# Thirty-five products that nobody reads, ahead of ten steps of a front written out by hand

## Chip, cores, metric

One core of a Trainium2 chip runs the whole program. The time is the device time of one execution in microseconds (us), and the figure given is the median of several runs. The engines are TensorE (PE in the rows; PEld are its weight loads), VectorE (DVE), ScalarE (ACT), GpSimd (POOL) and SyncE (SP, which issues most DMAs).

## What is computed

The reference is a block with two halves, cut here to its last lines:

```python
    x = A_u
    mod = (_silu(c) @ w_mod).reshape(c.shape[0], 6, 1, -1)
    sa, ca, ga, sb, cb, gb = (mod[:, 0], mod[:, 1], mod[:, 2], mod[:, 3], mod[:, 4], mod[:, 5])
    h = _layernorm(x, axis=-1) * (1 + ca) + sa
    x = x + ga * _A_ref(h, A_A_re, A_A_im, A_B_re, A_B_im, A_C_re, A_C_im, A_log_dt, A_Dskip)
    h = _layernorm(x, axis=-1) * (1 + cb) + sb
    x = x + gb * _B_ref(h, B_w1, B_w3, B_w2)
    return x
```

`_A_ref` is a state-space layer: for each of 640 channels a kernel K of 2048 steps is made out of 128 complex exponentials and is convolved with the layer's input by Fourier transforms. `_B_ref` is a gated feed-forward layer (640 to 1728 and back). The sequence has 2048 rows.

## The kernel before

The first layer has 40 steps (numbered s or k, 16 channels each). A step makes tables of exponentials (words `PA`, `PQ` on PE; `XA`, `XQ`, the phases `AB`, `CO`, `SI` on ScalarE; `E1`, `E2`, `A1`, `A2` on VectorE), multiplies and sums them on PE into K (`kg`, function `kgen`, into the PSUM tile `pk`), scales K on VectorE (`D`, `K`, functions `k_direct` and `k1evac`: from `pk` to the SBUF tile `K1`, named `K` in the rows), transforms it on PE (`pt`, function `k_stage1`, into the PSUM tile `pt`) and copies the result on ScalarE into `uk` (`uk`, function `k_out`). The tables E and the PSUM tiles are scarce: there are two buffers of E, one `pk` and one `pt` (its bank is called "pb"), so that a step of each kind waits for the reader of the step before.

Beside that, the 16 blocks of the input (`U+0` to `U+15`) are normalised on ScalarE (`LN`) and transformed on PE (`U`, function `u_products`, into two PSUM tiles `pu`, one in the banks "Z", the other in the banks "A" or "B", which the tables' products `pa` use too), and each half is taken out of PSUM by ScalarE or VectorE (`V0`, `V1`, function `u_out`).

The front of the program, about its first 122 us, is one hand-written list of words, `FRONT` (L1017). While it runs, every instruction of every engine is kept in the order of that list (class `InOrder`, L105; L115 is the line of its helper, and so the line of nearly all rows). Each engine takes its instructions strictly in that order, and an instruction that waits holds up all behind it on its engine. The list's end, around the change, reads:

```python
        "A2+4 V0+10 V1+10 kg+4 R7+2 LG+3 LN+7 K+4 PA+8 E1+5 uk+3 XA+8 pt+4 E2+5 A1+5 XA+9 uk+4 PA+10 A2+5 "
        "E1+7 XA+11 U+15 LN+6 V0+15 PH+8 V1+15 kg+5 U+13 XA+10 pt+2 AB+8 E1+6 V0+13 V1+13 K+5 A1+6 A1+7 E2+6 "
        "PQ+8 E2+7 uk+2 XQ+8 U+12 XQ+9 V0+12 V1+12 U+14 A2+7 CO+8 V0+14 kg+7 A2+6 pt+5 V1+14 CL+0 K+7 kg+6 "
        "PH+10 E1+8 SI+8 ul+0 ul+3 PQ+10 AB+10 E1+9 SI+10 K+6 uk+5 ul+1 XQ+11 pt+7 XQ+10 uk+7 E2+8 A1+9 CO+10 "
        "pt+6 A1+8 uk+6 E2+9 A2+8 A2+9 ul+2 kg+8 st+10 PH+12 K+8 "
```

After the front, rounds of the same words and of the convolution (`st`, PSUM tile `p` in the rows; `kc` takes it out on ScalarE) go to about 345 us, and the second layer, dense products on PE, runs to the end. Where the first layer ends the kernel already has 16 products of a tile of zeros that nobody reads (L1157, tile `idle`), 128x128 weights and 512 columns each.

Of the kernel before, what the change touches and what calls it, by code (L numbers as in the profile page):

```python
# [120 lines left out]
def tile_kernel(ctx: ExitStack, tc: tile.TileContext, a):  # L121
    nc = tc.nc
    V, S, G, PE = nc.vector, nc.scalar, nc.gpsimd, nc.tensor
# [19 lines left out]
    V, S, G, PE, Q = (InOrder(tc, e, (front,)) for e in (nc.vector, nc.scalar, nc.gpsimd, nc.tensor, nc.sync))  # L143

    def keep(ins):

        return tc.keep_in_program_order(ins) if in_order[0] else ins
# [48 lines left out]
    lx = once([P, KD, 4, P], F32R, "lx")  # L196
    r2 = once([P, 8, NB], F32R, "r2")
# [326 lines left out]
    def u_products(j):  # L524

        x = xt[j]
        ut[j] = pus = [psS.tile([P, 2, 512], F32, name="pu", tag=t, bufs=1) for t in ("Z", "AB"[j % 2])]
        for h in range(2):
            one = j % 2 == 0 and h == 0
            for q in range(2 if one else 0):  # L530
                for hh in range(2):
                    PE.matmul(pus[h][hh * 64:hh * 64 + 64, q, :320], c1[q * NA:q * NA + 1],
                              rrow[q * NA:q * NA + 1, hh * 320:hh * 320 + 320],
                              start=True, stop=False, tile_position=(q * NA, hh * 64))
            for q in range(2):
                r0 = (2 * h + q) * NA
                r = slice(r0, r0 + NA)
                for hh in range(2):
                    PE.matmul(pus[h][hh * 64:hh * 64 + 64, q, :320], s1r[r], x[r, hh * 320:hh * 320 + 320],
                              start=not one, stop=True, tile_position=(r0, hh * 64))  # L540
# [14 lines left out]


    LAG = SPC + 2

    ph, cs, AA, EC, PK, K1 = {}, {}, {}, {}, {}, {}

    pA, pQ = {}, {}

    banks = {"A": ("zt", LAG), "Z": None, "B": None}
    used = {}

    def two_banks(shape, name, release):

        free = [t for t, r in banks.items() if r is None or r in used]
        tag = min(free, key=lambda t: used.get(banks[t], -1))
        banks[tag] = release  # L570
        return psS.tile(shape, F32, name=name, tag=tag, bufs=1)
# [95 lines left out]
    def kgen(s):  # L667
        E, A = EC.pop(s), AA.pop(s)
        pk = psS.tile([P, SD // 4, NB], F32, name="pk", tag="pk", bufs=1)
        for g in range(SD // 4):  # L670
            for st, x in enumerate((E, A)):
                for dq in range(4):
                    keep(PE.matmul(pk[dq * 32:dq * 32 + 32, g, :], x[:, g * 4 + dq, 1, :], x[:, g * 4 + dq, 0:3:2, :],
                                   start=(st == 0), stop=(st == 1), tile_position=(0, dq * 32)))
        PK[s] = pk
# [14 lines left out]
    def k_stage1(s):  # L690
        pt = PT[s] = psS.tile([P, 4, P], F32, name="pt", tag="pb", bufs=1)
        kk = K1.pop(s)
        for g in range(4):
            for c in range(2):
                keep(PE.matmul(pt[c * 64:c * 64 + 64, g, :], kk[:, g, :], s1[:, c, :],
                               start=True, stop=True, tile_position=(0, c * 64)))
# [45 lines left out]
    def stage2(ch, g):  # L742
# [7 lines left out]
        if n:  # L750
            p2 = two_banks(shape, "p2", ("zt", n + LAG))
        else:
# [99 lines left out]
    def late_products(g):  # L852

        zt, w = ztl[g], i2bt[g - LATE].rearrange("p (f c) -> p f c", f=4)
        for f in range(4):
            for j in range(4):
                r = slice(j * 32, j * 32 + 8)
                end = keep_order(PE.matmul(pls[j][:, :P], w[r, f, :], zt[r, f, :],
                                           start=(g == LATE and f == 0), stop=(g == 7 and f == 3),
                                           skip_group_check=True, tile_position=(j * 32, 0)))  # L860
        return end
# [92 lines left out]
    def conv_part(fn):  # L954
        return lambda k: fn((k - LAG) // 8, (k - LAG) % 8)

    parts = {"PH": phases, "AB": absph, "CO": cosine, "SI": sine, "PA": lambda k: exp_fast((k,)), "XA": fast,
             "PQ": lambda k: exp_slow((k,)), "XQ": slow, "E1": real1, "E2": real2, "A1": imag1, "A2": imag2,
             "kg": kgen, "D": k_direct, "K": k1evac, "pt": k_stage1, "uk": k_out}
    conv = {"st": conv_part(stage2), "kc": conv_part(k_copy), "T": conv_part(products), "P": conv_part(products2), "Y": conv_part(sums),  # L960
            "iv": conv_part(inverse1), "zt": conv_part(z_store)}
# [3 lines left out]
    def do(name, k):  # L965

        lo, hi = (LAG, LAG + 8 * NDC) if name in conv else (0, NS)
        if name in by_two and k % 2:
            return None
        if front[0]:  # L970
            assert (name, k) not in done and lo <= k < hi, (name, k)
        if (name, k) in done or not lo <= k < hi:
            return None
        done.add((name, k))
        used[name, k] = len(used)
        return (conv if name in conv else parts)[name](k)
# [20 lines left out]
    def u_first(i):  # L997

        u_load(0, i)
        if i == 0:  # L1000
            ahead[0, 1, "s2"] = stage2_load(1)
            for g in range(2):
# [3 lines left out]
    once_only = lambda fn: lambda k: fn()  # L1006
    fronts = {"wl": mod_load, "xl": ln1_load, "ms": mod_first, "mc": mod_cols, "LS": ln1_stats, "LG": ln1_power, "LN": ln1_norm,
              "U": u_products, "V0": lambda k: u_out(k, 0),
              "V1": lambda k: u_out(k, 1), "SA": once_only(shift_a), "SB": once_only(shift_b), "SC": once_only(shift_c),
              "SD": once_only(shift_d), "MG": once_only(gate_a), "MH": once_only(gate_b), "dc": once_only(small_loads),  # L1010
# [38 lines left out]
    for word in FRONT:  # L1049
        name, k = word[:2].rstrip("+"), int(word[len(word[:2].rstrip("+")):])  # L1050
# [36 lines left out]
    for rnd in range(8 + 1):  # L1087
        if 2 <= rnd < 7:
            late_load(rnd - 2)
        for word in ROUND if rnd < 8 else LAST:  # L1090
            name, k = word.split("+")
            k = int(k) + (EB * rnd if rnd < 8 else 0)
# [13 lines left out]

    for tk in range(NS + 1, LAG + 8 * NDC + 2):
        do("st", tk)
        do("kc", tk)
        if tk == LAG + 8 * NDC:  # L1110
            end, made = late_products(6), []
# [66 lines left out]
    V, S, G, PE = (InOrder(tc, e, (in_order,)) for e in (nc.vector, nc.scalar, nc.gpsimd, nc.tensor))  # L1178
# [612 lines left out]
```

## Time and profile before

| | |
|---|---|
| time, median of 3 runs | 910.67 us (909.97 to 912.61) |
| the profiled execution's own time | 908.64 us |
| its span, first to last instruction | 906.8 us |
| mean granted TensorE clock | 0.971 of full speed |
| PE, DVE, ACT, POOL busy | 860.9, 686.3, 537.5, 275.4 us |

A share of busy time is an average over the front, the rounds and the second layer, which have different limits. PEclk is the clock that the chip granted to TensorE: 1.00 is 2.4 GHz and 0.50 is 1.2 GHz, and a value between them is a mean over a stretch that holds both. A matmul's row in the timeline is longer than the distance to the next one's start, since they overlap; costs are therefore read from starts. Products of 32-bit floats stand in the rows twice (x16 for 8 instructions); the type float32r stands once.

### The profile page before, as it was taken

Reading aid. Unit: us, or ns where it says so; the run is one execution under the profiler, and the core shown is the slowest. Engines: PE = TensorE matmul, PEld = TensorE weight load, DVE = VectorE, ACT = ScalarE, POOL = GpSimd, SP = SyncE. Lnnn points to the kernel's source line nnn. Section 1 sums busy time; section 2 is a strip of 40 time slices with the busy share of each in tenths; the row PEclk is TensorE's granted clock in tenths of the full one; section 3 lists DMA queues with packets and bytes.
Section 4 is the critical chain, followed back from the end, with each engine's and each line's share of the span. In section 5 each row is a group of like instructions: output and inputs, shape, how many; then the busy total and the mean of one; then the engine's idle time right before and its main releaser. Section 6 shows DMA issues by size and latency. Waiting matters only on the chain.

```text
span 906.8 us, 20206 instructions
## 1 busy us (share of the span) xinstructions
PE 860.9 (95%) x8082; PEld 660.1 (73%) x8082; DVE 686.3 (76%) x1210; ACT 537.5 (59%) x762; POOL 275.4 (30%) x315
## 2 busy tenths in 40 slices
PE   3788979999999999999999999999999999999997
PEld 2445557776666767788888887788888888888886
DVE  5899899999999968786666556867866766653664
ACT  6989899999999535554343324665534333323432
POOL 3342544554443030422222103300522222100662
PEclk9677699999999999999999999999999999999999
DMA  9655387676665887862211169736311311223352
GB/s 270 213 219 190 147 242 224 196 207 196 207 210 189 282 253 235 212 211 73 59 56 40 51 157 265 226 109 205 100 59 59 116 44 44 59 102 101 102 199 77
DMA packets 106017, 140.69 MB, mean 155 GB/s; under 512 B 19940, under 2 KB 65508, under 8 KB 105924
## 3 DMA queue, kind: packets, MB, share of 16 engines
q1 hardware_dynamic: 95796, 115.29, 42.0%
q10 hardware_dynamic: 8272, 18.16, 6.7%
q0 software_dynamic: 1856, 5.97, 2.0%
q8 instruction: 63, 1.03, 0.5%
q14 instruction: 30, 0.25, 0.1%
HBM read 107.92 MB, written 31.46 MB: 154 GB/s over the span
## 4 chain that ended last, share of the span: by engine, by line
PE 70%; ACT 12%; DVE 11%; DMA 3%; issue 3%; POOL 0%; DVEq 0%; SPq 0%; ACTq 0%
PE ps L115 60%; PE p L115 5%; ACT A L115 3%; DVE A L115 3%; ACT cs L115 3%; DVE E L115 2%; ACT L115 1%; DVE uk L115 1%; PE pk L115 1%; DMA zs<-zt 1%; ACT ph L115 1%; ACT uk L115 1%; PE pt L115 1%; PE pu L115 1%; DVE u L115 1%
## 5 line engine op out<-in xcount | busy, mean ns | idle before, releaser
L115 DVE TENSOR_TENSOR s<-ps,s 128x512 f32<-128x512 f32 x138 | 94.8, 687 | 83.1 <-PE ps L115 82.9
L115 ACT CAST gh<-rw 128x640 fp32r<-128x640 f32 x87 | 63.2, 727 | 110.0 <-PE ps L115 84.2
L115 DVE TENSOR_TENSOR gl<-rw,gh 128x640 fp32r<-128x640 f32 x87 | 77.2, 887 | 62.9 <-ACT gh L115 60.3
L115 POOL TENSOR_TENSOR S<-rw 128x256 f32<-128x256 f32 x46 | 36.1, 787 | 229.2 <-DVE S0l L115 156.2
L115 POOL TENSOR_TENSOR ph<-thi,iota 128x1376 int32<-128x1376 int32 x20 | 56.3, 2817 | 108.9 <-DVE A L115 35.3
L115 PE MATMUL ps<-xA,gh 128*128 128x512 f32 x280 | 87.5, 391 | 0.4 <-ACT xA L115 0.4
L115 PE MATMUL ps<-gh,uh 128*128 128x512 f32 x224 | 87.6, 391 | 0.0
L115 PE MATMUL ps<-gl,uh 128*128 128x512 f32 x224 | 87.4, 390 | 0.0
L115 DVE TENSOR_TENSOR E<-A,cs 128x1024 f32<-128x1024 f32 (+1 forms) x80 | 82.0, 1037 | 2.1 <-PE pk L115 1.5
L115 PE MATMUL ps<-gh,ul 128*128 128x512 f32 x208 | 81.2, 390 | 0.0
L115 PE MATMUL p<-uk,s 128*64 128x256 f32 x576 | 70.7, 386 | 2.6 <-ACT zt L115 1.1
L115 ACT ACTIVATE A<-pa 128x1024 f32<-128x1024 f32 (+1 forms) x80 | 64.6, 847 | 3.6 <-PE pa L115 3.1
L115 PEld LDWEIGHTS ps<-xA,gh 128*128 128x128 f32 x280 | 52.3, 188 | 12.6 <-ACT xA L115 0.7
L115 POOL TENSOR_TENSOR rw<-rw,gbr 128x128 f32<-128x128 f32 x56 | 35.7, 668 | 73.9 <-DMA rw<-in_w_dram 72.9
L115 PEld LDWEIGHTS p<-uk,s 128*64 128x64 f32 x576 | 38.7, 137 | 25.6 <-ACT A L115 3.3
L115 PE MATMUL ps<-xA,gl 128*128 128x512 f32 x140 | 54.6, 390 | 0.0
L115 ACT ACTIVATE s<-ps 128x512 f32<-128x512 f32 (+1 forms) x33 | 19.7, 596 | 49.9 <-PE ps L115 47.1
L115 PE MATMUL pt<-s,K 128*64 128x128 f32 x640 | 45.7, 287 | 3.4 <-ACT uk L115 3.0
L115 PEld LDWEIGHTS ps<-gh,uh 128*128 128x128 f32 x224 | 42.1, 188 | 8.9 <-DVE h L115 0.2
L115 PEld LDWEIGHTS ps<-gl,uh 128*128 128x128 f32 x224 | 42.1, 188 | 8.9
L115 DVE TENSOR_TENSOR A<-A,ph 128x1024 f32<-128x1024 f32 x40 | 48.5, 1216 | 0.0
L115 POOL TENSOR_TENSOR rs<-mv,epst 128x1 f32<-128x1 f32 (+1 forms) x17 | 6.0, 354 | 132.9 <-DVE mv L115 128.0
(224 smaller groups left out, 2220.1 us busy)
## 6 DMA issues: line engine op xcount, KB each, us to landing
rw<-in_w_dram ACTq DMA_DIRECT2D x44, 320.0 KB, 3.1
us<-u SPq DMA_DIRECT2D x16, 640.0 KB, 3.2
rw<-in_wg_dram SPq DMA_DIRECT2D x31, 320.0 KB, 2.7
s<-in_s_dram SPq DMA_DIRECT2D x36, 256.0 KB, 3.9
i<-in_i_dram SPq DMA_DIRECT2D x36, 256.0 KB, 4.5
rw<-in_wu_dram SPq DMA_DIRECT2D x28, 320.0 KB, 3.2
uk<-us SPq DMA_DIRECT2D x16, 512.0 KB, 4.9
zs<-zt SPq DMA_DIRECT2D x16, 512.0 KB, 4.3
```

Source lines behind the costliest of these rows:

```text
L115: ins = fn(*args, **kw)
```

## The change

A table names ten steps and a number for each. Ahead of such a step's products, PE makes that many products of two tiles that are long at hand, `lx` (as weights, 128 rows and 128 columns) and `r2` (512 columns, 256 where the bank has no more), into the very PSUM bank that the step's own products are about to overwrite. 21 of the 35 are 512 columns wide, and 14, those ahead of K products, are 256 wide. Nothing else is added, removed or moved.

```diff
@@ u_products(j)
         ut[j] = pus = [psS.tile([P, 2, 512], F32, name="pu", tag=t, bufs=1) for t in ("Z", "AB"[j % 2])]
+        idle_first("U", j, pus[0][:, 0])
@@
     LAG = SPC + 2
 
+    idle_products = {("U", 15): 2, ("kg", 5): 5, ("U", 13): 2, ("pt", 2): 2, ("U", 12): 2, ("U", 14): 3,
+                     ("kg", 7): 3, ("pt", 7): 4, ("pt", 6): 6, ("kg", 8): 6}
+
+    def idle_first(name, k, bank):
+        for _ in range(idle_products.get((name, k), 0)):
+            keep(PE.matmul(bank, lx[:, 0, 0, :], r2.rearrange("p j b -> p (j b)")[:, :bank.shape[1]], start=True, stop=True))
+
@@ kgen(s)
         pk = psS.tile([P, SD // 4, NB], F32, name="pk", tag="pk", bufs=1)
+        idle_first("kg", s, pk.rearrange("p g b -> p (g b)"))
@@ k_stage1(s)
         kk = K1.pop(s)
+        idle_first("pt", s, pt.rearrange("p g c -> p (g c)"))
```

PE's order in the changed program, from the last `pa` ahead of `U+15` to `pt+2`. In brackets are the engines that a row waits for (Activation is ScalarE); `r_98,lx` are the new products, and rows left out are the rest of `kg+5` and `U+13`.

```order
L115 MATMUL pa<-r_98,lx 128x512 [waits Activation_49]
L115 MATMUL pu<-r_98,lx 128x512 x2
L115 MATMUL pu<-x,misc 64x320 x4
L115 MATMUL pu<-x,misc 64x320 [waits Activation_49]
L115 MATMUL pk<-r_98,lx 128x256 x5
L115 MATMUL pk<-E 32x64 [waits DVE_49]
L115 MATMUL pu<-r_98,lx 128x512 [waits DVE_49]
L115 MATMUL pt<-r_98,lx 128x512 x2
L115 MATMUL pt<-s_74,K_938 64x128 x8
```

The steps keep their order; the new products stand ahead of each, and those of `U+13` take over the wait for VectorE that the step's own first product had.

PE's order before, from `PQ+10` to `kg+8` (`pt+7`, `pt+6`, then the first products of `kg+8`):

```order
L115 MATMUL pa<-r_99,lx 128x256 x4
L115 MATMUL pt<-s_74,K_1224 64x128 [waits Activation_49]
L115 MATMUL pt<-s_74,K_1224 64x128 x7
L115 MATMUL pt<-s_74,K_1286 64x128 [waits DVE_49,Activation_49]
L115 MATMUL pt<-s_74,K_1286 64x128 x7
L115 MATMUL pk<-E 32x64 [waits DVE_49]
L115 MATMUL pk<-E 32x64 x3
L115 MATMUL pk<-A 32x64 [waits DVE_49]
```

The same place in the changed program:

```order
L115 MATMUL pa<-r_99,lx 128x256 x4
L115 MATMUL pt<-r_98,lx 128x512 [waits Activation_49]
L115 MATMUL pt<-r_98,lx 128x512 x3
L115 MATMUL pt<-s_74,K_1243 64x128 x8
L115 MATMUL pt<-r_98,lx 128x512 [waits Activation_49]
L115 MATMUL pt<-r_98,lx 128x512 x5
L115 MATMUL pt<-s_74,K_1305 64x128 [waits DVE_49]
L115 MATMUL pk<-r_98,lx 128x256 x6
L115 MATMUL pk<-E 32x64 [waits DVE_49]
L115 MATMUL pk<-A 32x64 [waits DVE_49]
```

The wait for ScalarE, which frees the bank of `pt`, has gone from the transform's first product to the first new one, so the new products stand behind that wait and the transform stands behind them.

## Rows read from the trace of the kernel before

**Rows 1.** Busy time by stretch: us, engine busy (instructions), granted PE clock, DMA share, GB/s.

```profile
94.40:95.70 1.30, 1.05 (x12) 0.55 (x8) 1.30 (x3) 1.30 (x3) 0.00 (x0) 1.00 0.05 13
95.70:102.50 6.80, 6.80 (x106) 3.45 (x106) 5.98 (x7) 5.58 (x6) 5.15 (x3) 0.50 0.24 96
102.50:105.90 3.40, 2.69 (x44) 1.48 (x42) 3.37 (x6) 2.36 (x5) 1.30 (x1) 0.99 0.48 186
105.90:112.80 6.90, 6.90 (x102) 4.24 (x104) 5.56 (x10) 6.89 (x5) 3.28 (x2) 0.51 0.49 186
112.80:122.20 9.40, 5.07 (x170) 3.87 (x166) 7.97 (x11) 9.31 (x11) 2.88 (x3) 1.00 0.83 228
...
125.00:290.00 165.00, 162.16 (x3128) 115.02 (x3116) 161.05 (x278) 164.46 (x184) 77.27 (x41) 1.00 0.67 207
...
345.00:906.00 561.00, 555.33 (x2798) 452.31 (x2792) 374.25 (x647) 238.90 (x414) 139.20 (x214) 1.00 0.41 118
```

**Rows 2.** Timeline of PE: start us, us, line operation out<-in, [idle before <-releaser].

```profile
96.06 2.54 PE L115 MATMUL pu<-x,misc 32*64 32x320 f32 x16
...
98.52 0.44 PE L115 MATMUL pk<-E 128*32 128x64 f32 x8
...
100.39 1.37 PE L115 MATMUL pu<-x,misc 32*64 32x320 f32 x16
101.69 1.49 PE L115 MATMUL pt<-s,K 128*64 128x128 f32 x16
...
106.89 2.60 PE L115 MATMUL pu<-x,misc 32*64 32x320 f32 x16
109.42 0.44 PE L115 MATMUL pk<-E 128*32 128x64 f32 x8
...
111.29 1.80 PE L115 MATMUL pt<-s,K 128*64 128x128 f32 x16
113.02 0.32 PE L115 MATMUL pk<-E 128*32 128x64 f32 x8
...
114.05 0.39 PE L115 MATMUL pa<-r,lx 32*128 32x256 f32 x4
115.71 1.09 PE L115 MATMUL pt<-s,K 128*64 128x128 f32 x16 [1.26 <-ACT uk L115]
118.58 1.09 PE L115 MATMUL pt<-s,K 128*64 128x128 f32 x16 [1.78 <-ACT uk L115]
119.60 0.32 PE L115 MATMUL pk<-E 128*32 128x64 f32 x8
121.10 0.32 PE L115 MATMUL pk<-A 128*32 128x64 f32 x8 [1.18 <-DVE A L115]
```

**Rows 3.** Timeline of ACT: the idle time of 95 to 124 us and what follows it.

```profile
103.22 0.58 ACT L115 COPY uk<-pt 128x512 f32<-128x512 f32 x1 [1.70 <-PE pt L115]
...
105.09 0.69 ACT L115 COPY u<-pu 128x640 f32<-128x640 f32 x1 [0.29 <-PE pu L115]
...
115.09 0.57 ACT L115 COPY uk<-pt 128x512 f32<-128x512 f32 x1
...
117.93 0.59 ACT L115 COPY uk<-pt 128x512 f32<-128x512 f32 x1
...
121.66 0.56 ACT L115 COPY uk<-pt 128x512 f32<-128x512 f32 x1
...
124.27 0.59 ACT L115 COPY kc<-p 128x512 f32<-128x512 f32 x1 [0.23 <-PE p L115]
```

**Rows 4.** Timeline of DVE: its waits for PE in 109 to 123 us.

```profile
111.42 0.17 DVE L115 TENSOR_TENSOR pk<-pk,dz 128x4 f32<-128x4 f32 x1 [1.04 <-PE pk L115]
...
114.07 2.37 DVE L115 TENSOR_TENSOR E<-A,cs 128x1024 f32<-128x1024 f32 x1 [0.89 <-PE pk L115]
...
122.16 0.17 DVE L115 TENSOR_TENSOR pk<-pk,dz 128x4 f32<-128x4 f32 x1 [0.51 <-PE pk L115]
```

**Rows 5.** Timeline of PE: the sixteen products of zeros that the kernel has already.

```profile
350.03 3.92 PE L115 MATMUL ps<-idle 128*128 128x512 f32 x16
```

## Prediction

> **What bounds the kernel now.** I read the stretches first, then the three engines' timelines around the change.
>
> The stretches show two falls of TensorE's clock where the new products go: 0.50 of full speed from 95.7 to 102.5 us and 0.51 from 105.9 to 112.8, with 0.99 between and 1.00 after [rows 1]. PE is busy for all of both low stretches, 6.80 of 6.80 and 6.90 of 6.90 us, so a busy PE did not keep the clock. Ahead of the first fall it was busy 1.05 of 1.30 us with small products on 32 rows and with `pt`. In the stretches it ran `pu` (32 rows), then `pk` and `pt` (128 rows), and each rise came behind those last [rows 2].
>
> What PE's pace costs shows on the others. ScalarE waits 1.70 us for `pt+2` and 0.29 for `U+12`; behind that, from 105.1 to 124.3, it has no gap [rows 3], and from 125 to 290 it is busy 164.46 of 165 us [rows 1]. VectorE waits 1.04, 0.89 and 0.51 us for `pk` [rows 4] and is then busy 161.05 of 165. PE itself is busy 162.16 of 165 there and 555.33 of 561 from 345 on [rows 1]. So three engines are nearly full behind the front: what the front ends later or earlier is carried to the end, but for the half microsecond that ScalarE has left. PE's waits of 1.26, 1.78 and 1.18 us near 115 to 121 cost nothing by themselves: PE waits there for ScalarE's copies and for VectorE's tables [rows 2].
>
> **The price of one new product.** Sixteen of the same size start from 350.03 and take 3.92 us with the last one's overlapping end, 0.39 by the same rows [rows 5]: (3.92 - 0.39)/15 = 0.235 us each, at full clock; I take 0.23. No row shows one at half clock. `pk`, the same 64 records, takes 1.03 us at full clock (113.02 to 114.05) and 1.87 at half (109.42 to 111.29, or 98.52 to 100.39) [rows 2], a factor of 1.8; a plain halving of the clock would be 2. So 0.41 to 0.46; I take 0.43. A 256-wide one has no row either: it costs at most a wide one, and half of one if columns set the time, 0.12 and 0.21, which I take. All 35 in the open would cost 21 x 0.23 + 14 x 0.12 = 6.5 us at full clock and 21 x 0.43 + 14 x 0.21 = 12 at half.
>
> The Trainium skill (TensorE: Matmul & The Clock Gate, Back-to-back issue gap) gives N/1.2 ns cold and N/2.4 + 2.5 warm, so 0.213 and 0.109 us at N = 256; by these the sums would be 11.9 and 6.1 us, and the forecast would not move.
>
> **Part one: `U+15`, `kg+5`, `U+13`, `pt+2`.** In the profiled execution the clock had fallen at 95.7, and the first new product can start only at 96.06, where `U+15` stood [rows 1, 2]: it comes too late to prevent that fall. I let the clock stay low until about 102.5 as before.
> - `U+15`: 2 x 0.43 = 0.86. Its second half waited about 0.1 us for ScalarE before, which covers that much. `pk` starts 0.8 late, near 99.3.
> - `kg+5`: 5 x 0.21 = 1.05, then 1.87 for `pk` as before: `U+13` is reached at 102.2, not 100.39.
> - `U+13`: two products across the rise, 0.55; its own 1.30 at half clock becomes about 0.7 at full: 103.5, not 101.69.
> - `pt+2`: 2 x 0.23, then 1.03 (the full-clock `pt` at 115.71 [rows 2]; 1.42 before): 105.0.
>
> ScalarE's copy behind `pt+2` stood at 103.22 after a wait [rows 3]. It now comes at 105.0, **1.8 us later**, and no gap follows on ScalarE in which to make that up.
>
> **Part two: `U+12`, `U+14`, `kg+7`.** Two, three and three products, 5 x 0.23 + 3 x 0.12 = 1.5 us at full clock. If they keep it, the second fall does not happen: the three pieces from 106.89 to 113.02 (the `x` products of `U+14`, `pk`, `pt`) shrink from 6.1 us to 6.1/1.8 = 3.4. Net PE gains 1.2. It buys ScalarE nothing, since that engine had no wait between 105.1 and 124.3 [rows 3]. It removes VectorE's waits of 1.04 and 0.89 [rows 4], which just pays for the 1.8 by which VectorE is late out of part one. So at `K+7` VectorE is on time, and ScalarE is 1.8 late.
>
> **Part three: `pt+7`, `pt+6`, `kg+8`.** All stand behind ScalarE. Its copy of 115.09 (0.57 long) frees the bank for `pt+7`, and 4 x 0.23 = 0.92 and 1.03 follow: the transform is done 1.95 after the copy, and ScalarE asks for it 2.3 after it (117.93 - 115.66), so this is covered. The copy of 117.93 frees the bank for `pt+6`: 6 x 0.23 = 1.38 and 1.03, 2.4 after the copy's end at 118.52; ScalarE asks at 121.66, 3.1 after. Covered too. What is not covered is the queue behind: `kg+8` follows with 6 x 0.12 = 0.72 and 1.03, so `pk` is complete 118.52 + 2.41 + 0.72 + 1.03 = 122.7, when ScalarE is on time; before it was 122.16, since its wait for A ended at 121.10 [rows 2, 4]. That is +0.5, and with ScalarE 1.8 late it is **+2.3**: VectorE's `D+8` and `K+8`, and PE's first convolution product behind it, are that late, and ScalarE's next copy (124.27) with them.
>
> **Sum.** From 122 us all three engines are 1.8 to 2.3 us late; I take 2.3 less the half microsecond of rest that ScalarE has until 290: +1.8, carried to the end. The profiled execution's own time is 908.64 us (span 906.8, 1.84 around it), 2.0 under the median of 910.67. The sum against it is 908.64 + 1.8 = 910.4; against the median, which the runs of the changed kernel will be set against, 910.67 + 1.8 = **912.5**. About 0.3%, 2.7 us, is what a measurement of this kernel can tell from no change, so the forecast is a small loss that counts as no change. Its own range is 911.2 to 914.5: the +0.5 of part three alone, up to 2.3 with no rest on ScalarE and the 1.5 of part two's products on top, if the second fall comes all the same (+3.8).
>
> **Rivals.**
>
> *The clock holds from the first product on, and ScalarE's waits shrink.* The Trainium skill says in TensorE: Matmul & The Clock Gate (Part 1: The HAM clock gate) that the throttled state is the default and that sustained matmul activity releases it; by that rule more dense products where PE ran thin hold the clock at full. In this case's rows PE busy for 6.8 us on end stayed at half [rows 1], so busy time as such did not do it, but sixteen wide products on 128 rows at 350 ran at full clock [rows 5]. The time: at full clock `pt+2` would end near 102.0 even with its idle products (96.06 + 0.46 + 1.2 + 0.6 + 1.03 + 0.46 + 0.7 + 0.46 + 1.03), 1.2 earlier than 103.18, which is inside ScalarE's wait of 1.70. Part three takes 0.5 back. Result -0.7 to -1.2, so 909.7; if both waits of ScalarE went (1.70 + 0.29) it would be -2.0, 908.7. For it: the fall at 95.7 may come elsewhere in other executions, whose times spread by 2.6 us. Against: in the one execution shown the fall is ahead of the first new product.
>
> *A third low stretch: slower by more than a measurement's doubt.* Late by 2 us, PE waits longer for ScalarE near 115 to 121, and if the clock falls there, the dense work from 122 on starts at half. Price: a low stretch of 6.9 us holds work for 6.9/1.8 = 3.8, so it costs 3.1, and PE is nearly full there, with nothing to absorb it. 910.67 + 1.8 + 3.1 = 915.6. The point from which it decides is a granted clock below 1.00 anywhere between 113 and 130 us. Against: before, PE was busy only 5.07 of 9.40 us from 112.8 to 122.2 and the clock stayed at 1.00 [rows 1]; ten wide and six narrow products go just there. For: in the first part the new products run at half clock, cost double, and can also prolong that stretch past 102.5, at the same price.
>
> *The products do nothing that counts.* They fall into waits that are there anyway (1.26, 1.78, 1.18 us [rows 2]) and the clock falls and rises as before or a little sooner: what part one costs, the rise gives back. 910.7.
>
> **Chances.** Forecast 0.45; third or longer low stretch 0.27; clock held 0.20; nothing 0.08. Slower by over 2.7 us (over 913.4): all of the second, and 0.13 of the forecast's 0.45, 0.40. Faster by over 2.7 (under 907.9): only the clock held, with both waits of ScalarE gone and a fall avoided that the profiled execution did not have, 0.07. The rest, 0.53, is no change. A range of 908.8 to 916.2 takes in the held clock's lower value and the third stretch with a little over; about 2 in 10 stay outside.
>
> **What would show it.** In the changed kernel's stretches: the granted clock from 96 to 113. Half until about 102 and full after it is the forecast, full throughout the first rival, low anywhere behind 113 the second. On ScalarE's timeline: the copy behind `pt+2` near 105 and no gap after it, or near 102. On VectorE's: no wait for `pk` near 111 and 114, and a longer one than 0.51 us at `D+8`. On PE's: `kg+8` directly behind its idle products and no longer waiting for A. The forecast is wrong if ScalarE's copy behind `pt+2` is on time or early, or if the rounds behind 125 us absorb the lateness, which the full engines speak against.

## The result, and the profile after

The changed kernel took 916.64 us (median of 15 runs, 912.66 to 922.6) beside 912.01 for the kernel before on the same chip (15 runs, 909.97 to 914.47): a ratio of 1.005, 95% interval 1.0033 to 1.0066, slower by 3.0 to 6.0 us. A second comparison gave 916.21 against 912.90: 1.0037, 1.0011 to 1.0064. The forecast was 912.5, a loss of 1.8, and its wide range ended at 916.2. Of the 4.1 us between forecast and result, 1.3 is the base: more runs of the kernel before have a median of 912.0, not 910.67. The other 2.8 is a loss that was sized too small.

The profiled execution of the changed kernel took 915.29 us (span 913.5, mean clock 0.975). By stretch, with the columns of [rows 1], the changed kernel:

```profile
95.70:102.50 6.80, 6.80 (x113) 3.68 (x109) 5.35 (x6) 5.96 (x6) 4.99 (x3) 0.68 0.14 59
102.50:105.90 3.40, 3.40 (x47) 2.10 (x44) 3.12 (x6) 1.38 (x3) 1.53 (x1) 1.00 0.42 167
105.90:112.80 6.90, 6.09 (x155) 3.89 (x141) 6.33 (x11) 6.18 (x6) 2.33 (x1) 1.00 0.47 191
112.80:122.20 9.40, 5.22 (x82) 3.80 (x72) 8.86 (x10) 8.00 (x9) 4.48 (x4) 0.82 0.84 238
```

The low stretch that [rows 1] shows from 105.9 to 112.8 is gone: the clock is 1.00 there. A new one has come behind it (0.82 from 112.8 to 122.2); in half-microsecond steps it lies from 117.1 to 120.5. PE's timeline of the changed kernel shows where, with the columns of [rows 2]; the operands `r,lx` at 128x512 and 128x256 are the new products:

```profile
101.33 0.74 PE L115 MATMUL pu<-r,lx 128*128 128x512 f32 x2
101.99 0.79 PE L115 MATMUL pu<-x,misc 32*64 32x320 f32 x16
...
107.53 0.96 PE L115 MATMUL pu<-r,lx 128*128 128x512 f32 x3 [0.81 <-ACT u L115]
108.42 0.77 PE L115 MATMUL pu<-rrow,misc 1*64 1x320 f32 x8
...
113.51 0.39 PE L115 MATMUL pa<-r,lx 32*128 32x256 f32 x4
117.39 2.08 PE L115 MATMUL pt<-r,lx 128*128 128x512 f32 x4 [3.49 <-ACT uk L115]
119.40 1.61 PE L115 MATMUL pt<-s,K 128*64 128x128 f32 x16
121.70 1.67 PE L115 MATMUL pt<-r,lx 128*128 128x512 f32 x6 [0.69 <-ACT uk L115]
123.30 1.09 PE L115 MATMUL pt<-s,K 128*64 128x128 f32 x16
124.33 0.97 PE L115 MATMUL pk<-r,lx 128*128 128x256 f32 x6
125.23 0.32 PE L115 MATMUL pk<-E 128*32 128x64 f32 x8
```

PE waits 3.49 us for ScalarE's copy, the clock falls in that wait, and the four products of `pt+7` start at half clock: 2.01 us from start to start, where the forecast had 0.92. ScalarE and VectorE of the changed kernel:

```profile
104.52 0.58 ACT L115 COPY uk<-pt 128x512 f32<-128x512 f32 x1 [2.40 <-PE pt L115]
...
106.78 0.69 ACT L115 COPY u<-pu 128x640 f32<-128x640 f32 x1 [0.69 <-PE pu L115]
...
116.77 0.57 ACT L115 COPY uk<-pt 128x512 f32<-128x512 f32 x1
121.06 0.58 ACT L115 COPY uk<-pt 128x512 f32<-128x512 f32 x1 [1.33 <-PE pt L115]
```

```profile
111.59 0.17 DVE L115 TENSOR_TENSOR pk<-pk,dz 128x4 f32<-128x4 f32 x1 [0.54 <-PE pk L115]
...
126.40 0.17 DVE L115 TENSOR_TENSOR pk<-pk,dz 128x4 f32<-128x4 f32 x1 [4.70 <-PE pk L115]
```

The last row is `D+8`. It stood at 122.16 [rows 4], so it is 4.24 late, and the rows say where the time lies. ScalarE's copy of `pt+5` is 1.68 late (116.77 against 115.09 [rows 3]). From that copy to the one of `pt+7` it was 2.84 us and is 4.29, with a wait of 1.33 for `pt+7`: 1.45. From there to `D+8` it was 4.23 and is 5.34: 1.11. Together 4.24. The own time differs by 6.65, and the other 2.4 come behind the front, 1.4 of them in one pause of PE near 229 us that no releaser explains. How much of all this belongs to the change, one execution of each kernel can't tell; it is the subject of the second set of experiments.

### The profile page after: what moved, and what is told of

Its sections match the earlier page's. It is cut to its first block, busy times and chain, and to the rows that moved or that the text cites. A ratio compares the mean times of both kernels' runs of the same rounds, so it can differ in the third digit from the quotient of the medians.

```text
span 913.5 us, 20274 instructions
## 1 busy us (share of the span) xinstructions
PE 867.4 (95%) x8117; PEld 666.1 (73%) x8117; DVE 684.7 (75%) x1210; ACT 537.9 (59%) x762; POOL 276.7 (30%) x315
## 3 DMA queue, kind: packets, MB, share of 16 engines
q8 instruction: 64, 1.05, 0.5%
## 4 chain that ended last, share of the span: by engine, by line
PE 73%; ACT 10%; DVE 10%; DMA 3%; issue 2%; SPq 1%; DVEq 0%; ACTq 0%
PE ps L115 58%; PE p L115 8%; ACT A L115 3%; PE pt L115 3%; ACT cs L115 2%; DVE A L115 2%; PE pk L115 2%; DVE u L115 2%; DVE uk L115 1%; ACT ph L115 1%; DMA s<-in_s_dram 1%; ACT L115 1%; DVE E L115 1%; PE pm L115 1%; DMA A<-zs 1%
```

## The experiments

In the kernels below only products that nobody reads differ; none leaves work out. Edits are against the changed kernel. The letters of the theories are those of each expectation. Two thoughts run through them. One says that the order costs: the products of part three stand behind ScalarE's copies in PE's order, and part one makes ScalarE late. Its rivals: the added instructions as such, TensorE's added time as such, or the clock.

### Which products cost

One part each, then pairs, then all but a few:

```
part one   idle_products = {("U", 15): 2, ("kg", 5): 5, ("U", 13): 2, ("pt", 2): 2}
part two   idle_products = {("U", 12): 2, ("U", 14): 3, ("kg", 7): 3}
part three idle_products = {("pt", 7): 4, ("pt", 6): 6, ("kg", 8): 6}
```

> The products of part one alone (U+15 2, kg+5 5, U+13 2, pt+2 2). Theory Q (each product costs its time on PE, and steps queued behind pass the delay to ScalarE, which is full): the copy behind pt+2 about 1.3 to 1.8 us late, and the time 1.3 to 1.8 us (0.15 to 0.2%) above before. Theory C (the loss is that the clock falls a third time, near 117, while PE waits in its queue): part one adds no wait there, so within 0.5 us of before, on average over runs, or a gain if the early low stretch gets shorter.

> The products of part two alone (U+12 2, U+14 3, kg+7 3). Q: they fall in a stretch where ScalarE has no wait and VectorE has 1.9 us of waits for PE; between -0.5 and +1.0 us. C: the second fall (near 106) is prevented in executions that have it, but a fall is only put off to the next thin stretch near 117: 0 to +1.5 us, and low stretches later than in before.

> The products of part three alone (pt+7 4, pt+6 6, kg+8 6). Q: kg+8 ends 0.5 us later than in before, so +0.5 us, in every run. C: the dense products near 115 to 121 prevent the fall there, which the slower ones of the runs of before would have: -0.5 to -2 us on average, with a smaller spread than before. Were part three the whole loss of the change by itself, +4.6 us.

> Parts one and two without part three (19 products). If the loss adds up by part, this is the sum of the two single ones, and the rest of the change's 4.6 us is part three's: Q +1.8 to +2.8 here. If it is part three that turns lateness into loss (its idle products hold kg+8 behind a copy of ScalarE that is late), this one is near +1 and the full change far above the sum of parts.

> Parts two and three without part one. The theory after the first runs (L): part three costs more the later ScalarE is, since kg+8 follows ScalarE's copies of pt+7 and pt+6 through the idle products, while before it had the wait for A to absorb lateness: +0.5 us with ScalarE on time, +2.1 us with ScalarE 1.5 us late or more, and on top a half-clock price if the clock is low there. Without part one ScalarE is late only where the early stretch makes it so by itself: between 0 and +2 us. If instead any two parts together are free (only all three lose), 0.

> The change without the six narrow products ahead of kg+8. L: kg+8 ends 0.7 us earlier than in the full change; the wide ones ahead of pt+7 and pt+6 stay in the chain from ScalarE's copies to kg+8: about 3 to 3.5 us of the 4.6 stay. C (a product there guards the clock): the clock is guarded by ten wide ones, so the same as the full change.

> The change without the ten wide products ahead of pt+7 and pt+6. L: kg+8 loses 1.4 us (pt+6) and, where the clock is low or ScalarE waits for pt+7, up to 1 us more: about +1.5 us or less stays of the 4.6. C: the clock falls near 117 more often than in the full change, so no better than it.

> Parts one and three without part two (U+12, U+14, kg+7). Theory A, part one makes ScalarE late and part three's products stand behind ScalarE, so the two together make the loss: +4 to +5 us against the kernel before, as with all 35 products, since part two only added 0.1. Theory B, the loss is the sum of many small costs in no particular place: part one's 1.2 and part three's 0.2, so +1 to +2.

Measured (12 runs each, 15 and 12 of the whole; beside them the kernel before with 29 to 35 runs, median 912.54 to 912.90, and 15 at 912.01 beside the first of the whole):

| products | median, us | ratio to before [95%] |
|---|---|---|
| part one | 914.26 | 1.002 [1.0001, 1.0039] |
| part two | 913.35 | 1.0003 [0.9985, 1.0021] |
| part three | 913.41 | 1.0003 [0.9984, 1.0021] |
| one and two | 912.77 | 1.0007 [0.9987, 1.0026] |
| two and three | 914.38 | 1.0023 [1.0, 1.0046] |
| one and three | 914.91 | 1.0021 [0.9999, 1.0042] |
| all but `kg+8` | 915.47 | 1.0025 [1.0003, 1.0048] |
| all but `pt+7`, `pt+6` | 913.59 | 1.0012 [0.9991, 1.0032] |
| all | 916.64, 916.21 | 1.005 [1.0033, 1.0066], 1.0037 [1.0011, 1.0064] |

Part one alone costs about what was forecast, though its interval is barely clear of nothing. Part three alone costs nothing that can be seen; a pair that contains it costs about half of the whole. One and two were expected 1.8 to 2.8 us slower if the lateness alone cost, and gave 0.0 by the medians and 0.6 by the ratio. All but `kg+8` was expected at 3 to 3.5 us and gave 2.3 by the ratio. One and three were expected at 4 to 5 us by the theory of the order and at 1 to 2 by its rival, a sum of small costs: they gave 2, so this run speaks for the rival, or part two isn't free beside the others; its interval overlaps that of the second comparison of the whole. The intervals are 0.2% to either side, which leaves it open whether the parts simply add up (1.2 + 0.1 + 0.2 by the means, against 3 to 5 for all) or make each other worse.

### Instructions, TensorE's time, or the order

The same 35 places with products of 32 rows, 32 weight columns and 32 columns; with full weights and 32 columns; the whole change with the ten wide products of `pt+7` and `pt+6` in the banks "Z", which ScalarE doesn't hold; and products only where PE was idle anyway:

```diff
 e9 (NA is 32)
-            keep(PE.matmul(bank, lx[:, 0, 0, :], r2.rearrange("p j b -> p (j b)")[:, :bank.shape[1]], start=True, stop=True))
+            keep(PE.matmul(bank[:NA, :NA], lx[:NA, 0, 0, :NA], r2.rearrange("p j b -> p (j b)")[:NA, :NA], start=True, stop=True, tile_position=(0, 0)))
 e5
+            keep(PE.matmul(bank[:, :32], lx[:, 0, 0, :], r2.rearrange("p j b -> p (j b)")[:, :32], start=True, stop=True))
 e10, e18
+        if s in (6, 7):
+            idle_first("pt", s, psS.tile([P, 2, 512], F32, name="pi", tag="Z", bufs=1)[:, 0])
-        idle_first("pt", s, pt.rearrange("p g c -> p (g c)"))
+        if s < 6:
+            idle_first("pt", s, pt.rearrange("p g c -> p (g c)"))
 e11 (wide products alone, in place of the 35; the first in PA+8, then ahead of kg+4, U+14, and pt+7 and pt+6)
+            if s == 9 and n == NB:
+                idle_in("Z", 2)
+        if s == 4:
+            idle_in("Z", 4)
+        if j == 14:
+            idle_in("pb", 3)
+        if s in (6, 7):
+            idle_in("Z", 4)
```

> All 35 products in their places with 32 rows, 32 weight columns and 32 moving columns each. The 32-column products of before still loaded 128x128 weights and took 0.14 to 0.25 us each on PE, as long as the 256-wide ones, so that run did not take PE's time away; this one does (a weight load of 32 columns). If PE's time is what the loss is made of: within 0.15% of before. If it is the places, the waits or 35 more instructions: the 0.5% of the change.

> All 35 products in their places, each 32 columns wide instead of 512 or 256: the waits move to the new products as in the change, but they take almost no time on PE and hardly work. If the loss is PE's time in the queue (Q) or what the dense products do to the clock (C), this is within 0.15% of before. If it is the places themselves (35 more instructions, a wait taken over by another instruction), the loss of the change, 0.5%, stays.

> The full change, but the ten wide products ahead of pt+7 and pt+6 go into the banks Z, which are free by then, instead of the transform's own bank: they need no longer wait for ScalarE's copies and run in PE's idle time before those. L: the chain from ScalarE's copies to kg+8 is shorter by about 1.1 us at pt+7 and 1.6 at pt+6, so about 1 to 1.5 us of the change's 4.6 stays (as in the run without those ten), and the clock does not fall at 117 in the profile. If the ten cost by their mere number, as much as the change.

> All 35 products, with the ten wide ones of pt+7 and pt+6 in a bank that ScalarE doesn't hold, so that they can run during the waits for ScalarE's copies. Theory A, the order behind ScalarE's copies is what costs: 0 to +1 us, clearly under the kernel with all 35. Theory B, TensorE's added time as such costs: +4 to +5, as with all 35.

> All 35 products again, on the same chip and beside the same runs of the kernel before as the next kernel. Both theories +4 to +5 us (ratio 1.004 to 1.006); a ratio under 1.002 would say that the first comparison overstated the loss.

> A version that only fills PE's idle time: 4 wide products into banks Z ahead of kg+4 (PE idles 1.09 us there), 2 between the halves of PA+8 (0.51 us), 3 into the transform's bank ahead of U+14 (0.71 us), 4 into Z ahead of pt+7 and 4 ahead of pt+6 (1.26 and 1.78 us). L: nearly nothing on the path (at most +0.5 us), and the clock falls less often, the first two groups stand ahead of the fall at 95.7: -1 to -2.5 us against before, to about 911. If dense products in the gaps do not hold the clock: +0.5 us.

| kernel | median, us | ratio to before [95%] |
|---|---|---|
| e9, tiny products | 913.02 | 0.9998 [0.998, 1.0015] |
| e5, full weights, 32 columns | 917.32 | 1.0046 [1.0023, 1.007] |
| e10, ten wide ones in another bank | 912.64 | 1.0003 [0.9983, 1.0023] |
| e18, the same again, beside e17 | 913.42 | 1.0008 [0.9987, 1.0029] |
| e17, all 35 as in the change | 916.21 | 1.0037 [1.0011, 1.0064] |
| e11, only in idle times | 912.72 | 0.9999 [0.9983, 1.0016] |

Thirty-five more instructions in these places cost nothing that can be seen (e9). e5 was expected within 0.15% of the kernel before if PE's time or the clock made the loss, and it lost as much as the change. But it doesn't take PE's time away, as was meant. PE's timeline of e5:

```profile
119.89 0.62 PE L115 MATMUL pt<-r,lx 128*128 128x32 f32 x4
120.44 1.09 PE L115 MATMUL pt<-s,K 128*64 128x128 f32 x16
122.77 1.32 PE L115 MATMUL pt<-r,lx 128*128 128x32 f32 x6 [1.23 <-ACT uk L115]
124.03 1.98 PE L115 MATMUL pt<-s,K 128*64 128x128 f32 x16
125.93 1.46 PE L115 MATMUL pk<-r,lx 128*128 128x32 f32 x6
127.33 0.44 PE L115 MATMUL pk<-E 128*32 128x64 f32 x8
```

Four take 0.55 us, 0.14 each; at half clock, from 125.93, six take 1.40, 0.23 each. Each product brings its own 128x128 weights. The Trainium skill (TensorE: Matmul & The Clock Gate, LDWEIGHTS) has the time of a weight load follow its columns and not its rows, by its formula 128/1.2 = 107 ns. The trace agrees in kind, with 0.14 us for the whole product here and 0.22 for four with 32 rows and 32 weight columns in e9 (118.29 to 118.51); at half clock it was longer.

From their start to that of the step behind them, with waits left out, the 35 take 8.0 us in this profile, 8.9 to 11.1 in the four of the changed kernel (below), and 3.3 in e9. The clock of e5 is lower besides: 0.962 on the mean of its 12 runs, 0.968 in the 35 of the kernel before beside them. So e5 can't tell PE's time from the clock.

e10 and e18 have all of the change's products too, and lose nothing that can be seen; their intervals lie below that of the first comparison of all 35, while e17's and e18's overlap; e17 itself came out a little under its expected 1.004 to 1.006. Taken together, the 24 runs of e10 and e18 have a mean of 913.4 us and the 27 of the whole 916.6: 3.2 less, 95% interval 1.6 to 4.7, on chips where the kernel before had medians of 912.0 to 912.9. Only the bank differs, and with it the wait: the ten wide products run before ScalarE's copy frees the transform's bank instead of after it. The clock doesn't differ: 0.973 and 0.974 on the mean of the runs of e10 and e18, 0.974 and 0.976 in those of the whole. That is the theory of the order, and a pair of executions shows the mechanism bare. In the second profile of the changed kernel (e12, below) and in that of e18 the clock fell at nearly the same times, 87.4 to 90.8 and 107.8 to 111.2 in e12, 87.7 to 91.1 and 108.1 to 111.5 in e18, and was full from there to 130. PE of the changed kernel in e12:

```profile
116.26 1.20 PE L115 MATMUL pt<-r,lx 128*128 128x512 f32 x4 [2.09 <-ACT uk L115]
117.38 1.09 PE L115 MATMUL pt<-s,K 128*64 128x128 f32 x16
119.16 1.65 PE L115 MATMUL pt<-r,lx 128*128 128x512 f32 x6 [0.68 <-ACT uk L115]
120.75 1.09 PE L115 MATMUL pt<-s,K 128*64 128x128 f32 x16
121.77 0.97 PE L115 MATMUL pk<-r,lx 128*128 128x256 f32 x6
122.67 0.32 PE L115 MATMUL pk<-E 128*32 128x64 f32 x8
```

and PE of e18:

```profile
114.40 1.20 PE L115 MATMUL pi<-r,lx 128*128 128x512 f32 x4
116.58 1.09 PE L115 MATMUL pt<-s,K 128*64 128x128 f32 x16 [0.98 <-ACT uk L115]
117.60 1.65 PE L115 MATMUL pi<-r,lx 128*128 128x512 f32 x6
119.45 1.09 PE L115 MATMUL pt<-s,K 128*64 128x128 f32 x16 [0.20 <-ACT uk L115]
120.48 0.98 PE L115 MATMUL pk<-r,lx 128*128 128x256 f32 x6
121.39 0.32 PE L115 MATMUL pk<-E 128*32 128x64 f32 x8
```

In e12 PE waits for the copy and then runs the idle products; in e18 they run inside that wait, which shrinks from 2.09 to 0.98 and from 0.68 to 0.20. ScalarE's copy of `pt+7` stands at 118.53 and 118.81, so e18 is even the later one there, and yet its `kg+8` starts 1.28 earlier (121.39 against 122.67). VectorE's `D+8` in e12 and in e18:

```profile
123.84 0.17 DVE L115 TENSOR_TENSOR pk<-pk,dz 128x4 f32<-128x4 f32 x1 [2.46 <-PE pk L115]
```

```profile
122.56 0.17 DVE L115 TENSOR_TENSOR pk<-pk,dz 128x4 f32<-128x4 f32 x1 [0.86 <-PE pk L115]
```

The own time of the two goes the other way, 912.09 us for e12 and 913.38 for e18: behind `D+8` single executions differ by more than this. And the profile of e10, an execution of 916.65 us, has a fall from 118.6 to 122.0 that its expectation ruled out, and `D+8` at 124.38 with a wait of 2.96.

Products only in idle times (e11) were expected to gain 1 to 2.5 us and change nothing that can be seen either. No version was measured as faster than the kernel before.

### One execution or the kernel

Both kernels were profiled again, unchanged:

> The changed kernel itself in a second profiled execution. Theory A, the third low stretch belongs to the change: TensorE's clock falls again between 116 and 119 us, and VectorE's D+8, which waits for the products of kg+8, starts at 125 us or later with a wait above 3 us. Theory B, the fall at 117.1 us was an accident of the one execution that was looked at: no low stretch between 113 and 123 us, and D+8 starts near 123.5.

> A third profiled execution of the changed kernel, with the expectation of the second: theory A a low stretch from 116 to 119 us and D+8 at 125 us or later; theory B no low stretch there and D+8 near 123.5.

> The kernel before in a second profiled execution. Its first one took 908.64 us, under every one of its later executions. If the start of D+8 is what the rest of the time hangs on, a slower execution of it, 911 to 914 us, has D+8 at 123.5 to 125 and not at 122.16. If the executions differ behind the front, D+8 stands within 0.5 us of 122.16 whatever the time.

> A third profiled execution of the kernel before: a second low stretch between 105 and 113 us and none from 113 to 123, as in the first, if the pattern belongs to the kernel; D+8 between 122 and 125 us, later in the slower execution.

The low stretches are worked out from the granted clock in steps of half a microsecond. `U+15` is the start of that step on PE, with its new products, and "copy" is the start of ScalarE's copy of `pt+5`, which frees the bank for `pt+7`. The start of `D+8` has its wait for `pk` beside it:

| execution | own time, us | low stretches between 93 and 130 us | `U+15` | copy | `D+8` (wait) |
|---|---|---|---|---|---|
| before, first | 908.64 | 95.7-102.5, 106.0-112.8 | 96.06 | 115.09 | 122.16 (0.51) |
| before, second (e13) | 916.67 | 98.0-104.8, 108.2-115.0, 121.9-125.3 | 98.12 | 118.24 | 125.53 (1.44) |
| before, third (e15) | 912.99 | 97.8-104.6, 108.0-114.8, 121.7-125.1 | 97.23 | 116.40 | 124.07 (1.24) |
| changed, first | 915.29 | 93.2-100.0, 117.1-120.5 | 96.62 | 116.77 | 126.40 (4.70) |
| changed, second (e12) | 912.09 | 107.8-111.2 | 96.47 | 115.64 | 123.84 (2.46) |
| changed, third (e14) | 924.78 | 97.4-104.2, 121.3-128.1 | 97.98 | 119.35 | 130.35 (6.06) |
| changed, fourth (e17) | 914.20 | 93.2-100.0, 117.1-120.5 | 96.23 | 116.55 | 126.26 (4.78) |

The falls are not the kernel's alone: they lie elsewhere in other executions of the same program. A low stretch behind 116 us came in two of three executions of the kernel before and in three of four of the changed one, so the expectation of a fall at 116 to 119 in each execution of the changed kernel fell with e12 and with e14, where it came at 121.3, and the fall at 117.1 can't be put down to the change. The expectation that the kernel before keeps its pattern fell with e13 and e15. The Trainium skill says something like it of the start of a kernel (TensorE: Matmul & The Clock Gate, Part 1: The HAM clock gate): how many products run at the low clock there differs from run to run of one kernel, with a penalty under 1% of a typical span. These executions show it of falls in the midst of one.

What does belong to the change stands in the same table. Low clock between 93 and 130 us falls from 13.6, 17.0 and 17.0 us to 10.2, 3.4, 13.6 and 10.2: the products do keep the clock up. The timed runs agree, with a mean granted clock of 0.974 in the 27 of the changed kernel and 0.969 in the 128 of the kernel before that list it. And VectorE's wait at `D+8` grows from 0.51, 1.44 and 1.24 us to 4.70, 2.46, 6.06 and 4.78. The mean start of `D+8` goes from 123.9 to 126.7, 2.8 later; the mean own time from 912.8 to 916.6. Over the 20 profiled executions of all kernels the start of `D+8` and the own time go together (correlation 0.88, 1.2 us of time for each us of `D+8`; without the four executions with `D+8` behind 129 it is 0.70 and 1.0).

The same 20 profiles can be sorted by both. From the copy of `pt+5` to `D+8` they took, in us:

| | clock full in it | clock falls in it |
|---|---|---|
| the ten wide products not there, or not behind ScalarE's copies | 7.07 (before), 7.19 (e11), 6.61 (e18) | 7.29 (e13), 7.67 (e15), 7.81 (e1), 7.14 (e2), 7.41 (e4), 8.00 (e8), 8.27 (e9), 7.90 (e10) |
| the ten wide products behind the copies | 8.20 (e12), 8.20 (e3) | 9.63 (first), 9.71 (e17), 9.79 (e16), 11.00 (e14), 11.22 (e7), 12.11 (e6) |

Left out is e5 with its narrow products, 10.05 with a fall. At full clock the products of part three cost 1.1 us here (8.20 against 7.07). A fall adds at most 1.2 where they don't stand behind the copies, and 1.4 to 3.9 where they do.

Why a fall costs the changed kernel more is seen in e14, its slowest execution. PE:

```profile
119.97 1.20 PE L115 MATMUL pt<-r,lx 128*128 128x512 f32 x4 [3.48 <-ACT uk L115]
121.10 1.82 PE L115 MATMUL pt<-s,K 128*64 128x128 f32 x16
123.60 2.93 PE L115 MATMUL pt<-r,lx 128*128 128x512 f32 x6 [0.68 <-ACT uk L115]
126.45 1.89 PE L115 MATMUL pt<-s,K 128*64 128x128 f32 x16
128.27 0.98 PE L115 MATMUL pk<-r,lx 128*128 128x256 f32 x6
129.18 0.32 PE L115 MATMUL pk<-E 128*32 128x64 f32 x8
```

and in PE of the kernel before in e13, with a fall at nearly the same time:

```profile
121.74 1.89 PE L115 MATMUL pt<-s,K 128*64 128x128 f32 x16 [1.78 <-ACT uk L115]
123.56 0.44 PE L115 MATMUL pk<-E 128*32 128x64 f32 x8
...
125.44 1.95 PE L115 MATMUL p<-uk,s 128*64 128x256 f32 x16
```

Before, `pt+6` and `kg+8` are through at 125.44, 3.70 us after PE could start on `pt+6`. In e14 the six idle products alone take 2.85 of that room (123.60 to 126.45), and `kg+8` only begins 5.58 after (129.18).

## Why the prediction was wrong

**The step that failed: what part three costs.** "What is not covered is the queue behind" was priced at +0.5 us, by two transforms that ScalarE would find ready. From ScalarE's copy of `pt+5` to `D+8` the three executions of the kernel before took 7.07, 7.29 and 7.67 us, the four of the changed one 9.63, 8.20, 11.00 and 9.71: 2.3 more on the mean. Two things make it up. With the clock full (e12) it is 1.1, 0.6 over the forecast, which is what the three groups cost beyond their price (next paragraph). The rest comes in the three executions in which the clock falls there: "so this is covered" fails, and ScalarE waits 1.33, 0.65 and 1.42 us for `pt+7`, in e14 also 1.62 for `pt+6`, where the kernel before has no wait.

**Wrong: the price.** At full clock two wide products with their place between small ones took 0.66 (101.33 to 101.99), three 0.89, six 1.60; six narrow ones 0.90 (124.33 to 125.23). That is 0.23 and 0.12 each, as taken from [rows 5], and about 0.2 more for each group, which the forecast left out. Ten groups add 2 us; with what ran at half clock the 35 take 10.3 us in the first profile, against 7.4 by the sum of the three parts' own terms.

**Too large: part one.** By the first profiles the copy behind `pt+2` came 1.30 late (104.52 against 103.22), against 1.8 forecast. But executions differ by as much ahead of the change: from the start of `U+15` that copy came after 7.16, 7.27 and 7.60 us before, and after 7.90, 6.90, 9.12 and 8.06 with the change, 0.7 later on the mean. At the copy of `pt+5` it is 0.8 (19.4 to 20.3 from `U+15`). So it was partly luck that the forecast for `D+8`, 2.3 late, is near the 2.8 of the mean: a part one that was priced 1.0 too high hid a part three that was priced 1.8 too low.

**Wrong: the half microsecond that ScalarE has left.** It was taken off the 2.3. The mean own time grew by 3.8, 1.0 more than the start of `D+8`; the time behind `D+8` lies between 786.5 and 791.1 us in the three executions of the kernel before, so that the 1.0 can't be told from nothing, but no rest shows.

**Wrong: that one execution's falls are the kernel's.** "I let the clock stay low until about 102.5 as before" took the falls of the one profile as a schedule. They move, and the profile of before was a good draw: of the 143 timed runs of that kernel that stand beside the experiments one is as low as its 908.64 us, and all others lie at 909.27 or above. The rival of a third low stretch was priced at 3.1 us and taken for a thing that the change might bring; the kernel before has such a stretch in two of three executions. What the change brings is the work that lies in it.

**Right: part two, and that its clock buys nothing.** The low stretch at 106 was gone in the first profile, and half as long or gone in the other three. VectorE's waits of 1.04 and 0.89 [rows 4] became 0.54 and none in the first profile, 1.61 and 0.17 in e12. No time that can be seen came of it (1.0003 for part two alone): ScalarE had no waits there to give back.

**The rivals.** That the clock holds and ScalarE's waits shrink failed in its second half. In e12 the clock was full from 92 to 104 us, and the copy behind `pt+2` came 6.90 us after `U+15`, only 0.26 sooner than in the first profile of before, where the clock was low, and not 1.2: the four groups ahead of it took 2.8 us, of which the rival had counted 2.0. That the products do nothing holds, as far as can be seen, of e9, e10 and e11, not of the change. "Carried to the end" held in kind: 1.2 us of time for each us at `D+8`, or 1.0.

Left open: whether the parts add up or make each other worse; a pause of PE near 230 us that no releaser ends, 0.77 to 1.36 us in the four executions of the changed kernel and at most 0.43 in the three of the kernel before (e9 and e10 have it too, 1.05 and 1.36, without a loss that can be seen); and why the clock fell at a given moment.

## What to carry to other kernels

Work that is meant to keep TensorE's clock up belongs into the engine's waits, not behind them: in a bank that nobody holds the same ten products cost nothing that could be seen (1.0003 and 1.0008), and behind a copy that frees the bank they lengthen the chain that everyone waits for, by 1.1 us at full clock and by more when the clock falls all the same. Ask first what a faster clock could give back there: with the next engine full, no version gained anything that could be seen. And one profile shows one draw of the clock's falls: profile the unchanged kernel two or three times before a sum is built on where they lie.

## What the runs showed that was not expected

- Three executions of the unchanged kernel had two, three and three low stretches between 93 and 130 us, those of the first at other times, with 908.64, 916.67 and 912.99 us.
- PE was busy for 6.80 of 6.80 us and still at 0.50 in [rows 1]; with small-column products on full weights (e5) it stayed low from 95.7 to 119.5 while it was busy for most of it:

```profile
95.70:102.50 6.80, 6.80 (x107) 4.78 (x105) 5.06 (x6) 5.41 (x6) 5.32 (x3) 0.50 0.23 96
102.50:105.90 3.40, 3.40 (x38) 2.37 (x22) 3.37 (x6) 0.20 (x1) 0.26 (x1) 0.50 0.02 5
105.90:112.80 6.90, 6.09 (x57) 3.08 (x53) 5.35 (x7) 5.05 (x6) 1.40 (x1) 0.50 0.47 191
```

- Four products of 32 columns with full weights took 0.55 us at full clock (e5, 119.89 to 120.44), 0.14 each; six of 256 columns 0.90, 0.15 each: narrower than 256 columns was no shorter.
- The spread grows with the change: its 15 runs lie within 9.9 us, the kernel before's 15 beside them within 4.5; in the second comparison its 12 lie within 12.2, the 29 beside them within 8.9. The 12 with products in idle times (e11) lie within 3.8.
